# Linear attention and two MLPs: the inverse root by one table function, and a Newton step with one pass less behind it

## The chip, the cores and the metric

The kernel runs on one core of one Trainium2 chip. The metric is the device time of one execution in microseconds (us). The core has five engines that work side by side, each through its own list of instructions in a fixed order: PE (TensorE, matrix products), ACT (ScalarE, table functions and copies), DVE (VectorE, elementwise passes), POOL (GpSimd) and SP (SyncE, which here issues most transfers). An instruction that has to wait for another engine holds up all that stands behind it on its own.

## The reference, cut to what matters

```python
q, k, v: (8, 8, 576, 64)                      # batch, heads, tokens, head size
kv  = einsum('bhsd,bhse->bhde', k, v)
out = einsum('bhsd,bhde->bhse', q, kv)
rms = sqrt(mean(out * out, axis=-1) + 1e-06)
x   = out / rms * g_norm                      # as 4608 x 512
h   = x @ w_in                                # 512 -> 2048
g   = h where h >= 1, 0 where h <= -1, else (h + 1)**2 / 4
x   = g @ w_out                               # 2048 -> 512
return relu(x @ w_in2)**2 @ w_out2            # second MLP
```

The change is in `out / rms`: how 1/rms is made and multiplied in.

## The kernel before, in words

The work goes by batch (8 blocks of 512 tokens; the 64 tokens left of each batch are kept in `xrem` for the end) and by pair of heads (`hp` 0 to 3, 128 rows for two heads). Three stretches follow each other. In the **opening** the attention of batch 0 is made alone (`kv_stage`, `t_first`, `o_first`, `r_first`), pair by pair; while that goes on, the first weight pieces are converted, and PE is given filler products (`pwarm`, L1157). In **layer 1** a loop over blocks and 16 slices of the hidden width runs `h_stage` (12 products into `ph`, then `u`), `g_stage` (split of `u` into a high and a low part, `gs`) and `out_stage` (products into `acc`); the attention of the next batch (`t_stage`, `o_stage`, `r_stage`) is woven in as hooks. The **second stretch** (lines from L794 on) has the last block and the second MLP, and no inverse root.

A float32 operand of a product is split into a high part (a cast, on ACT) and a low part (a subtraction, on DVE). A weight piece goes through four steps first: `raw` (ACT, L268), `d` in two passes (DVE, L270 and L271), then cast (ACT, L217) and subtraction (DVE, L185). The engines of each step are set in the tables ENGINES and ENGINES2 at the head of the file. The order of instructions on each engine is set by a scheduler from the order of the calls and their dependences; `tc.high_priority()` around `o_first` and `r_first` pulls those forward.

The inverse root, for one pair of heads: PE multiplies the squares with `ones` (two halves of 288 columns, `pr`); ACT takes Ln of each half (L535; L602 later), then Exp of -0.5 times that over 576 columns (L537; L604); ACT squares the result into `t` (`square`, L224). DVE then makes one Newton step on it: `newton` twice (L519, one for each half, reading `pr` again), `norm` in two passes over 576 columns (L522 and L523: first with the root `y`, then with `o`, which is the product `out` times -g/2). ACT and DVE split the result into `x`. `r_first` runs four times, `r_stage` 28 times. The table of Ln and Exp is loaded once, at the start (L1146).

PSUM, where products land, has 8 banks. In the opening `ph` of slices 2 to 5 lies in the four banks that `acc` takes over later: the first `acc` product can start only after DVE's pass `u` of slice 2 (L707) has read `ph` out of its bank.

Of the kernel before, what the change touches and what calls it, by code (L numbers as in the profile page):

```python
# [16 lines left out]

LN_SCALE = 2.0**-44  # L20
LN2 = 0.6931471805599453


# [54 lines left out]
def linear_attention_rms_two_mlps(  # L78
# [12 lines left out]
    nc = tc.nc  # L91
# [98 lines left out]
    lnb = const.tile([P, 1], F32, name="lnb")  # L190
    expb = const.tile([P, 1], F32, name="expb")
# [329 lines left out]
    def norm(t, y, o):  # L521
        nc.vector.scalar_tensor_tensor(t, t, -3.0, y, op0=ALU.add, op1=ALU.mult)  # L522
        nc.vector.tensor_tensor(t, o, t, ALU.mult)  # L523
# [3 lines left out]
    def r_first(hp):  # L527
        y, o = og.pop((0, hp))
        t = scratch(hp, "t")
        ms = []  # L530
        for half in range(2):
            ps = bank(0, f"pr_0_{hp}_{half}")
            m = ps[:, :U]
            nc.tensor.matmul(m, ones.bitcast(F32), y[:, half], start=True, stop=True)  # L534
            nc.scalar.activation(y[:, half], m, AF.Ln, bias=lnb, scale=LN_SCALE)  # L535
            ms.append(m)
        nc.scalar.activation(y, y, AF.Exp, bias=expb, scale=-0.5)  # L537
        square(engine("y", 0), t, y)
        for half in range(2):
            newton(t[:, half], ms[half])  # L540
        norm(t, y, o)
        n = TB // 2
        rem = xrem[0][:, hp, :].rearrange("p (h r) -> p h r", h=2)
        nc.gpsimd.tensor_copy(rem, t[:, :, n:])
        x = xs[1, 0][hp].rearrange("p a (h n) -> p a h n", h=2)
        marks.append(split(x, t[:, :, :n], "x", 0))
# [42 lines left out]
    def r_stage(b, hp):  # L589
# [6 lines left out]
        for half in range(2):  # L596
# [5 lines left out]
            nc.scalar.activation(y[:, c], m, AF.Ln, bias=lnb, scale=LN_SCALE)  # L602
            ms.append((c, m))
        nc.scalar.activation(y, y, AF.Exp, bias=expb, scale=-0.5)  # L604
        t = ap1.tile([P, S], F32, tag="wk2", name=f"t_{b}_{hp}")
        square(engine("y", b), t, y)
        for c, m in ms:
            newton(t[:, c], m)
        if b < LAST_B:
            norm(t, y, o)  # L610
# [4 lines left out]
        nc.vector.scalar_tensor_tensor(t, t, -3.0, y, op0=ALU.add, op1=ALU.mult)  # L615
        nc.vector.tensor_tensor(xt, o[:, :TB], t[:, :TB], ALU.mult)
        nc.vector.tensor_tensor(xrem[b][:, hp, :], o[:, TB:], t[:, TB:], ALU.mult)
# [528 lines left out]
    nc.scalar.preload_act_table_set("natural_log_exp_and_others")  # L1146
# [24 lines left out]
    nc.vector.memset(lnb, LN_SCALE * 1e-6)  # L1171
    nc.vector.memset(expb, -22.0 * LN2)
# [122 lines left out]
```

## Time and profile before

| | |
|---|---|
| median of 3 runs | 1556.57 us (1556.27 to 1558.22) |
| the profiled execution's own time | 1556.74 us |
| its span, first to last instruction | 1554.7 us |
| PE busy | 1545.8 us, 99% of the span |
| DVE busy | 1131.3 us, 73% |
| ACT busy | 909.6 us, 59% |

The span is 2.0 us shorter than the time of the same execution; the rest lies around it. The profiled execution stands 0.17 us over the median.

How to read it: busy shares are means over the whole span, and the three stretches are limited by different engines. A busy PE includes the time in which a product that has been issued passes through the array, so short waits can hide in it.

### The profile page before, as it was taken

The numbers are of one execution on the slowest core, as the hardware profiler recorded it, in microseconds if no ns is written. First come the engines' busy times: TensorE is split into PE (matmuls) and PEld (weight loads), VectorE is DVE, ScalarE is ACT, GpSimd is POOL, SyncE is SP. The second block draws the span as 40 slices with busy tenths as digits, with TensorE's granted clock in tenths as the row PEclk, the third lists the DMA queues.
The fourth block names the chain that finished last, engine by engine and source line by source line (L and its number), as shares of the span: only waits on it lengthen the run. The fifth ranks groups of instructions, "written<-read, shape, count | busy, mean of one in ns | idle before, by whom it ended". The sixth has DMA issues, their size and how long they took to land.

```text
span 1554.7 us, 22267 instructions
## 1 busy us (share of the span) xinstructions
PE 1545.8 (99%) x7727; PEld 1283.3 (83%) x7729; DVE 1131.3 (73%) x2000; ACT 909.6 (59%) x1713; POOL 20.5 (1%) x38
## 2 busy tenths in 40 slices
PE   9999999999999999999999999999999999999999
PEld 5787888888888888888888888888888888888898
DVE  6986886877877776754587559778965596558666
ACT  5977766767666676664355346456644463446354
POOL 0000000000000000000000000000000000000000
PEclk9999999999999999999999999999999999999999
DMA  9666899996877967935676867696876676877796
GB/s 288 197 216 187 278 319 279 304 313 197 274 250 238 284 208 227 293 98 172 193 245 194 227 213 246 197 238 200 259 227 204 205 238 197 241 248 224 212 392 249
DMA packets 327519, 368.22 MB, mean 237 GB/s; under 512 B 196976, under 2 KB 222576, under 8 KB 327408
## 3 DMA queue, kind: packets, MB, share of 16 engines
q1 hardware_dynamic: 295360, 308.60, 66.4%
q10 hardware_dynamic: 32048, 58.20, 9.9%
q8 instruction: 61, 1.00, 0.3%
q14 instruction: 50, 0.41, 0.1%
HBM read 282.59 MB, written 84.15 MB: 236 GB/s over the span
## 4 chain that ended last, share of the span: by engine, by line
PE 97%; ACT 1%; DVE 1%; issue 0%; DVEq 0%; ACTq 0%
PE po L878 27%; PE ph L878 27%; PE acc L238 20%; PE ph L238 19%; PE pkv L479 1%; PE po L238 1%; PE pr L601 1%; PE pwarm L1157 1%; ACT raw L268 0%; ACT w L217 0%; PE pr L534 0%; DVE t L519 0%; DVE w L185 0%; PE po L511 0%; DVE t L522 0%; PE po L569 0%
## 5 line engine op out<-in xcount | busy, mean ns | idle before, releaser
L878 PE MATMUL ph<-x,ws 128*128 128x512 f32 (+1 forms) x2016 | 422.4, 371 | 0.0
L878 PEld LDWEIGHTS ph<-x,ws 128*128 128x128 f32 x2016 | 355.8, 188 | 65.6
L878 PE MATMUL po<-t,ws 128*128 128x512 f32 x1680 | 381.6, 389 | 0.0
L878 PEld LDWEIGHTS po<-t,ws 128*128 128x128 f32 x1680 | 315.3, 188 | 65.5
L238 PE MATMUL ph<-x,w 128*128 128x512 f32 x1344 | 329.4, 392 | 1.3 <-ACT w L217 0.6
L238 PEld LDWEIGHTS ph<-x,w 128*128 128x128 f32 x1344 | 248.7, 188 | 54.3 <-ACT w L217 1.5
L807 DVE TENSOR_TENSOR t<-g,t 128x512 fp32r<-128x512 f32 (+1 forms) x288 | 183.3, 641 | 92.2 <-ACT t L217 84.6
L217 ACT CAST t<-g 128x512 fp32r<-128x512 f32 (+1 forms) x288 | 166.5, 585 | 101.8 <-PE po L878 50.2
L238 PE MATMUL acc<-gs,w 128*128 128x512 f32 x696 | 173.0, 392 | 1.5 <-DVE u L707 1.5
L238 PE MATMUL acc<-gs,wt 128*128 128x512 f32 x648 | 157.9, 391 | 0.0
L238 PEld LDWEIGHTS acc<-gs,w 128*128 128x128 f32 x696 | 128.6, 188 | 27.8 <-DVE u L707 1.9
L949 ACT ACTIVATE g<-h 128x512 f32<-128x512 f32 (+1 forms) x120 | 70.7, 589 | 119.8 <-DVE h L938 119.8
L238 PEld LDWEIGHTS acc<-gs,wt 128*128 128x128 f32 x648 | 120.1, 188 | 24.3
L705 ACT ACTIVATE u<-ph,halfb 128x512 f32<-128x512 f32 x112 | 77.2, 690 | 91.5 <-PE ph L238 89.1
L938 DVE CUSTOM_DVE_ANT_0 h<-ph,e 128x512 f32<-128x512 f32 (+1 forms) x120 | 76.4, 638 | 64.8 <-PE ph L878 57.3
L707 DVE SCALAR_TENSOR_TENSOR u<-u,ph 128x512 f32<-128x512 f32 x112 | 76.3, 681 | 54.2 <-ACT u L224 53.8
L928 DVE TENSOR_TENSOR e<-ph,e 128x512 f32<-128x512 f32 (+1 forms) x96 | 61.1, 643 | 50.2 <-PE ph L878 49.6
L230 DVE TENSOR_TENSOR gs<-u,gs 128x512 fp32r<-128x512 f32 x112 | 76.8, 686 | 22.2 <-ACT gs L217 21.8
L217 ACT CAST gs<-u 128x512 fp32r<-128x512 f32 x112 | 69.7, 622 | 37.5 <-DVE u L707 34.7
L224 ACT ACTIVATE u<-u 128x512 f32<-128x512 f32 x112 | 70.8, 632 | 1.4 <-ACT u L705 0.5
L217 ACT CAST x<-xr 128x512 fp32r<-128x512 f32 (+1 forms) x84 | 49.0, 586 | 36.0 <-DVE xr L858 17.5
L807 DVE TENSOR_TENSOR x<-xr,x 128x512 fp32r<-128x512 f32 (+1 forms) x84 | 53.1, 637 | 7.3 <-ACT x L217 7.3
(134 smaller groups left out, 1494.5 us busy)
## 6 DMA issues: line engine op xcount, KB each, us to landing
ws<-wsd SPq DMA_DIRECT2D x336, 512.0 KB, 4.2
wsd<-s ACTq DMA_DIRECT2D x96, 512.0 KB, 4.7
wt<-wsd SPq DMA_DIRECT2D x54, 512.0 KB, 5.4
raw<-in_moe_w_in_dram SPq DMA_DIRECT2D x32, 512.0 KB, 5.8
raw<-in_moe_w_out_dram SPq DMA_DIRECT2D x32, 512.0 KB, 6.2
xr<-x1d SPq DMA_DIRECT2D x36, 256.0 KB, 4.9
out_dram<-ov SPq DMA_DIRECT2D x142, 64.0 KB, 3.5
wsd<-w SPq DMA_DIRECT2D x17, 512.0 KB, 5.0
```

Source lines behind the costliest of these rows:

```text
L217: return e.copy(dst, src)
L224: e.activation(dst, src, AF.Square)
L230: lo = engine(op + "_lo", phase).tensor_tensor(t[:, 1, :], src, t[:, 0, :].bitcast(F32), ALU.subtract)
L238: nc.tensor.matmul(dst, wt(a), xt(c), start=first and n == 0, stop=last and n == 2)
L479: nc.tensor.matmul(ps[s, d], lhs, rhs, start=c == 0, stop=c == MR)
L705: nc.scalar.activation(u, ps, AF.Relu, bias=halfb, scale=0.5)
L707: nc.vector.scalar_tensor_tensor(u, u, 1.0, ps, op0=ALU.min, op1=ALU.max)
L807: engine2(op + "_lo").tensor_tensor(t[:, 1, :], src, t[:, 0, :].bitcast(F32), ALU.subtract)
L878: nc.tensor.matmul(ps, wt(a), xt(c), start=first and n == 0 and i == 0, stop=last and n == len(lhs) - 1 and i == 2, skip_group_check=True,)
L928: nc.vector.tensor_tensor(e[i, p], bank, e[i, 1], ALU.add)
L938: nc.vector._custom_dve(TENSOR_ADD_SAT, out=h, in0=bank, in1=add, s0=float("inf"), s1=0.0)
L949: nc.scalar.activation(g, h, AF.Square)
```

## The change

One function, `Abs_reciprocal_sqrt` of (mean + 1e-6), takes the place of Ln and Exp, and the table loaded at the start is the one that holds it. A new pass on DVE, `o = o * y`, comes ahead of `newton`; `norm` then has one pass, (t - 3) * o, in place of two. For the last batch that one pass writes its two destinations directly.

```diff
-            nc.scalar.activation(y[:, half], m, AF.Ln, bias=lnb, scale=LN_SCALE)
+            nc.scalar.activation(y[:, half], m, AF.Abs_reciprocal_sqrt, bias=epsb)
             ms.append(m)
-        nc.scalar.activation(y, y, AF.Exp, bias=expb, scale=-0.5)
         square(engine("y", 0), t, y)
+        nc.vector.tensor_tensor(o, o, y, ALU.mult)
         for half in range(2):
             newton(t[:, half], ms[half])
-        norm(t, y, o)
+        norm(t, t, o)
...
-    def norm(t, y, o):
-        nc.vector.scalar_tensor_tensor(t, t, -3.0, y, op0=ALU.add, op1=ALU.mult)
-        nc.vector.tensor_tensor(t, o, t, ALU.mult)
+    def norm(dst, t, o):
+        nc.vector.scalar_tensor_tensor(dst, t, -3.0, o, op0=ALU.add, op1=ALU.mult)
...
-        nc.vector.scalar_tensor_tensor(t, t, -3.0, y, op0=ALU.add, op1=ALU.mult)
-        nc.vector.tensor_tensor(xt, o[:, :TB], t[:, :TB], ALU.mult)
-        nc.vector.tensor_tensor(xrem[b][:, hp, :], o[:, TB:], t[:, TB:], ALU.mult)
+        norm(xt, t[:, :TB], o[:, :TB])
+        norm(xrem[b][:, hp, :], t[:, TB:], o[:, TB:])
...
-    nc.scalar.preload_act_table_set("natural_log_exp_and_others")
+    nc.scalar.preload_act_table_set("abs_reciprocal_sqrt_and_small")
```

`r_stage` is changed as `r_first` is. The scheduler lays the instructions out anew. Three places follow. In names such as `t_0_332` and `x_0_1_218` the last number is the buffer's; what stands ahead of it is the pair of heads, or batch (or matrix) and slice. The line numbers of the change are 8 to 11 lower.

First, DVE in the opening, from the pass `o` of pair 1 to the low part of `x` of pair 0. Before:

```order
L211 TENSOR_SCALAR o_1_349<-po_1_1_354,gvec 128x288
L519 SCALAR_TENSOR_TENSOR t_0_332<-pr_0_0_333,t_0_332 128x288
L519 SCALAR_TENSOR_TENSOR t_0_332<-pr_0_1_336,t_0_332 128x288
L185 TENSOR_TENSOR w_0_0_300<-d_0_0_297,w_0_0_300 128x2x256
L522 SCALAR_TENSOR_TENSOR t_0_332<-t_0_332,y_0_282 128x576
L271 SCALAR_TENSOR_TENSOR d_0_1_363<-raw_0_1_153,d_0_1_363 128x512
L523 TENSOR_TENSOR t_0_332<-o_0_283,t_0_332 128x576
```

The same engine and place in the change:

```order
L529 TENSOR_TENSOR o_0_281<-o_0_281,y_0_280 128x576
L511 SCALAR_TENSOR_TENSOR t_0_330<-pr_0_0_331,t_0_330 128x288
L511 SCALAR_TENSOR_TENSOR t_0_330<-pr_0_1_334,t_0_330 128x288
L263 SCALAR_TENSOR_TENSOR d_0_0_295<-raw_0_0_150,d_0_0_295 128x512
L203 TENSOR_SCALAR o_1_346<-po_1_1_351,gvec 128x288
L514 SCALAR_TENSOR_TENSOR t_0_330<-t_0_330,o_0_281 128x576
L178 TENSOR_TENSOR w_0_0_298<-d_0_0_295,w_0_0_298 128x2x256
L529 TENSOR_TENSOR o_1_346<-o_1_346,y_1_345 128x576
L222 TENSOR_TENSOR x_0_0_215<-t_0_330,x_0_0_215 128x512
```

The new product and the Newton passes of pair 0 have moved ahead of `o` of pair 1; the low part of the first weight, `w_0_0`, has moved behind the last pass of pair 0.

Second, ACT around the cast of `x` for pair 1. Before:

```order
L217 CAST x_0_0_217<-t_0_332 128x512
L512 ACTIVATE y_2_409<-po_2_0_411 128x288
L209 ACTIVATE o_2_410<-po_2_0_411,gvec 128x288
L535 ACTIVATE y_2_409<-pr_2_0_431,lnb 128x288
L217 CAST x_0_1_218<-t_1_393 128x512
L512 ACTIVATE y_2_409<-po_2_1_415 128x288
```

In the change:

```order
L209 CAST x_0_0_215<-t_0_330 128x512
L216 ACTIVATE t_1_390<-y_1_345 128x576
L209 CAST x_0_1_216<-t_1_390 128x512
L504 ACTIVATE y_2_405<-po_2_0_407 128x288
L201 ACTIVATE o_2_406<-po_2_0_407,gvec 128x288
```

The cast of `x_0_1` has moved ahead of the squares of pair 2 and of the first table function of pair 2.

Third, DVE where the first `acc` bank is freed (the pass `u` of slice 2). Before:

```order
L707 SCALAR_TENSOR_TENSOR u_0_1_612<-u_0_1_612,ph_0_1_599 128x512
L270 TENSOR_SCALAR d_1_4_635<-raw_1_4_518 128x512
L185 TENSOR_TENSOR w_1_3_596<-d_1_3_593,w_1_3_596 128x2x256
L230 TENSOR_TENSOR gs_0_1_625<-u_0_1_612,gs_0_1_625 128x512
L271 SCALAR_TENSOR_TENSOR d_1_4_635<-raw_1_4_518,d_1_4_635 128x512
L707 SCALAR_TENSOR_TENSOR u_0_2_654<-u_0_2_654,ph_0_2_641 128x512
```

In the change:

```order
L222 TENSOR_TENSOR gs_0_1_619<-u_0_1_606,gs_0_1_619 128x512
L178 TENSOR_TENSOR w_1_3_590<-d_1_3_587,w_1_3_590 128x2x256
L262 TENSOR_SCALAR d_1_4_629<-raw_1_4_512 128x512
L697 SCALAR_TENSOR_TENSOR u_0_2_648<-u_0_2_648,ph_0_2_635 128x512
L263 SCALAR_TENSOR_TENSOR d_1_4_629<-raw_1_4_512,d_1_4_629 128x512
```

The second pass of `d_1_4` has moved from ahead of `u_0_2` to behind it.

## Rows read from the trace of the kernel before

**Rows 1.** the page's head: span, busy us of each engine (share, instructions)

```profile
span 1554.7 us, 22267 instructions
PE 1545.8 (99%) x7727; PEld 1283.3 (83%) x7729; DVE 1131.3 (73%) x2000; ACT 909.6 (59%) x1713; POOL 20.5 (1%) x38
```

**Rows 2.** windows of all engines: stretch, us, busy us (instructions) of each, granted clock, DMA

```profile
27.00:38.00 11.00, 10.25 (x42) 7.34 (x42) 10.20 (x22) 7.51 (x16) 0.64 (x1) 1.00 0.95 330
38.00:57.30 19.30, 17.35 (x88) 12.65 (x87) 18.82 (x35) 18.99 (x37) 0.24 (x1) 1.00 0.91 273
57.30:100.00 42.70, 42.70 (x223) 34.60 (x222) 36.86 (x67) 36.73 (x74) 1.41 (x2) 1.00 0.56 162
100.00:700.00 600.00, 599.82 (x3150) 497.12 (x3148) 451.95 (x832) 411.86 (x817) 15.42 (x22) 1.00 0.80 250
700.00:1550.00 850.00, 850.00 (x4064) 717.55 (x4063) 597.57 (x1004) 421.11 (x747) 0.00 (x0) 1.00 0.74 229
```

**Rows 3.** PE's waits from 80 to 1550 us: waiter, releaser, us, times, longest

```profile
PE ph L238 <- ACT w L217: 0.2, 1, 0.2
```

**Rows 4.** timeline of PE: start, us, what [idle before, releaser]

```profile
1.19 4.73 PE L1157 MATMUL pwarm<-warm 128*128 128x512 bf16 x11 [1.19 <-DVE warm L1152]
...
6.46 1.47 PE L1157 MATMUL pwarm<-warm 128*128 128x512 bf16 x6
...
17.82 1.24 PE L534 MATMUL pr<-y,ones 128*128 128x288 f32 x4 [0.91 <-DVE t L519]
...
53.84 0.97 PE L238 MATMUL acc<-gs,w 128*128 128x512 f32 x3 [1.51 <-DVE u L707]
...
61.53 0.69 PE L479 MATMUL pkv<-v,k 128*64 128x64 f32 x16
```

**Rows 5.** windows of DVE alone: stretch, us, busy us (instructions)

```profile
12.83:53.71 40.88, 37.53 (x75) 1.00 0.95 294
```

**Rows 6.** timeline of DVE, opening: the gaps before u of slice 2

```profile
16.74 0.52 DVE L211 TENSOR_SCALAR o<-po,gvec 128x288 f32<-128x288 f32 x1 [0.98 <-ACT y L512]
...
26.13 0.69 DVE L230 TENSOR_TENSOR x<-t,x 128x512 fp32r<-128x512 f32 x1 [0.75 <-ACT x L217]
...
31.22 0.52 DVE L211 TENSOR_SCALAR o<-po,gvec 128x288 f32<-128x288 f32 x1 [0.67 <-ACT y L512]
...
48.98 0.69 DVE L185 TENSOR_TENSOR w<-d,w 128x512 fp32r<-128x512 f32 x1 [0.32 <-ACT w L217]
...
53.11 0.68 DVE L707 SCALAR_TENSOR_TENSOR u<-u,ph 128x512 f32<-128x512 f32 x1
```

**Rows 7.** timeline of ACT, opening: Ln and what it waits for

```profile
18.61 0.99 ACT L535 ACTIVATE y<-pr,lnb 128x288 f32<-128x288 f32 x2 [0.26 <-PE pr L534]
...
25.09 0.50 ACT L535 ACTIVATE y<-pr,lnb 128x288 f32<-128x288 f32 x1 [1.92 <-PE pr L534]
...
28.89 0.50 ACT L535 ACTIVATE y<-pr,lnb 128x288 f32<-128x288 f32 x1 [1.37 <-PE pr L534]
```

**Rows 8.** ACT's groups by shape: busy us, mean ns, idle before

```profile
L512 ACT ACTIVATE y<-po 128x288 f32<-128x288 f32 x8 | 3.3, 408 | 10.4 <-PE po L511 10.4
...
L535 ACT ACTIVATE y<-pr,lnb 128x288 f32<-128x288 f32 x8 | 3.9, 501 | 3.7 <-PE pr L534 3.7
...
L537 ACT ACTIVATE y<-y,expb 128x576 f32<-128x576 f32 x4 | 3.1, 776 | 0.1
...
L224 ACT ACTIVATE t<-y 128x576 f32<-128x576 f32 x4 | 2.7, 686 | 0.0
```

**Rows 9.** DVE's groups by shape, last passes of the opening

```profile
L522 DVE SCALAR_TENSOR_TENSOR t<-t,y 128x576 f32<-128x576 f32 x4 | 3.0, 753 | 0.0
...
L523 DVE TENSOR_TENSOR t<-o,t 128x576 f32<-128x576 f32 x4 | 3.0, 750 | 0.0
```

**Rows 10.** the raw weights to 75 us: transfers, issue to landing

```profile
DMA to landing us min/median/max: 4.4/8.1/11.2
```

**Rows 11.** the table load: count, ns, first and last start

```profile
L1146 ACT ACT_TABLE_LOAD  x1: 1283/1283/1283, 0.7 to 0.7; - x1
```

More of the change, by code (lines that the diff above doesn't have):

```diff
@@ L16 @@
 BF16 = mybir.dt.bfloat16
-LN_SCALE = 2.0**-44
-LN2 = 0.6931471805599453
 REBIAS = 2.0**-112
@@ L189, in linear_attention_rms_two_mlps @@
     gvec = const.tile([P, 1], F32, name="gvec")
-    lnb = const.tile([P, 1], F32, name="lnb")
-    expb = const.tile([P, 1], F32, name="expb")
+    epsb = const.tile([P, 1], F32, name="epsb")
     halfb = const.tile([P, 1], F32, name="halfb")
@@ L601, in r_stage @@
                 nc.tensor.matmul(m, one, s2[:, c], start=n == 0, stop=n == len(products) - 1)
-            nc.scalar.activation(y[:, c], m, AF.Ln, bias=lnb, scale=LN_SCALE)
+            nc.scalar.activation(y[:, c], m, AF.Abs_reciprocal_sqrt, bias=epsb)
             ms.append((c, m))
-        nc.scalar.activation(y, y, AF.Exp, bias=expb, scale=-0.5)
         t = ap1.tile([P, S], F32, tag="wk2", name=f"t_{b}_{hp}")
         square(engine("y", b), t, y)
+        nc.vector.tensor_tensor(o, o, y, ALU.mult)
         for c, m in ms:
@@ L609, in r_stage @@
         if b < LAST_B:
-            norm(t, y, o)
+            norm(t, t, o)
             nc.gpsimd.tensor_copy(xrem[b][:, hp, :], t[:, TB:])
@@ L1170, in linear_attention_rms_two_mlps @@
     nc.vector.tensor_scalar_mul(gvec, gvec, -0.5)
-    nc.vector.memset(lnb, LN_SCALE * 1e-6)
-    nc.vector.memset(expb, -22.0 * LN2)
+    nc.vector.memset(epsb, 1e-6)
     nc.vector.memset(halfb, 0.5)
```

## The prediction

> **What bounds the kernel now.** I read the head of the page first: PE is busy for 1545.8 of 1554.7 us, so what the change does to ACT and DVE counts only where PE waits for them [rows 1]. The windows say where that is. From 57.3 us on PE is busy without a break: 42.70 of 42.70, 599.82 of 600 and 850 of 850 us, at a granted clock of 1.00, which is the 2.4 GHz level [rows 2]. The waits of PE from 80 to 1550 us are a single one of 0.2 us [rows 3]. Twenty-eight of the 32 inverse roots are made there, on engines that have slack: ACT is busy for 411.86 and DVE for 451.95 of the 600 us from 100 to 700 [rows 2]. Taking 28 Exp away there is worth nothing, since PE's own list of products covers it. If that cover went, 28 Exp at 0.78 us, the opening's price [rows 8], would be 22 us.
>
> That leaves the opening, up to the first `acc` product. Between 38 and 57.3 us ACT is busy for 18.99 and DVE for 18.82 of 19.30 us, PE for 17.35 [rows 2]: here the two elementwise engines set the pace. The last long wait of PE ends it: the `acc` product starts at 53.84 us after 1.51 us of idleness, released by DVE's pass `u` [rows 4], which begins at 53.11 and takes 0.68 us [rows 6]. Whatever makes that pass earlier makes the end earlier by as much, as long as PE, which has no gap behind it, stays fed.
>
> So the question is what holds DVE up before that pass. From 12.83 us (the pass `o` of pair 0, whose inputs the change does not touch) to 53.71, where the engine passes on from `u` of slice 2, DVE is busy for 37.53 of 40.88 us: 3.35 us of gaps [rows 5]. Four of them make 2.72 us: 0.98, 0.75, 0.67 and 0.32, each a wait for ACT [rows 6]. The other 0.63 us is in gaps too short to be listed there.
>
> **The change part by part.** *The root.* No row shows it. Ln, with the same operands (a half of 288 columns out of PSUM, a bias from a column), takes 0.50 us; the square of the same half, without that column, 0.41 [rows 8]. I take 0.50; the bounds are 0.41 and, as if it were an Exp over twice the columns, 0.78. At 0.78 the 8 roots of the opening would cost ACT 8 x 0.28 = 2.2 us more, at 0.41 0.7 us less. The Trainium skill (ScalarE activation tables: per-element evaluation and per-set limits, "What a function is on this engine") says that with the same operands an activation costs the same whichever table is read; by it the 0.50 stands.
>
> *Exp goes.* Four in the opening at 0.78 us: ACT sheds 3.1 us [rows 8]. That is no gain by itself, because DVE does not shed anything.
>
> *DVE.* One pass over 576 columns (L523, 0.75 us) is replaced by the product `o*y` of the same shape and type; the other (L522, 0.75 us) stays with another operand [rows 9]. I take the difference as 0; being four passes of each, a tenth more on one of them would be 4 x 0.075 = 0.3 us. The last batch has the split pass in the other place, with as many columns. What is queued behind the new product on DVE are the two `newton` passes; they need ACT's square of the root, 0.69 us [rows 8], which runs while the product does. So the product delays them by under 0.1 us.
>
> *The gaps, from the order shown.* First gap (0.98, `o` of pair 1 waits for ACT's square of that pair): in the change the product of pair 0 and its `newton` passes stand ahead of it. Exp's place on ACT is taken by the square of the root, so they are ready about 0.7 us after the last root and bring some 0.75 + 0.75 us of work (two halves are one pass of 576 columns). The gap is filled: +0.98. Price: the low part of `w_0_0` now stands behind the last pass of pair 0 on DVE and needs a cast that stands on ACT behind the first root of pair 1. That root's product waited 0.91 us on PE for `newton` [rows 4], which the change lifts, so it starts at 16.9 instead of 17.82; ACT reads it 0.79 us later (18.61 less 17.82 [rows 4, 7]), at 17.7. Root and cast, about 0.9 us, bring the low part to 18.6. DVE gets there at 16.74 + 0.52 + 0.75, about 17.9. A new gap of 0.7.
>
> Second gap (0.75, low part of `x_0_1` waits for its cast): on ACT that cast stood behind a Ln that waited 1.92 us for PE [rows 7]; now it stands ahead of pair 2. +0.75. Third gap (0.67, `o` of pair 3): ACT's square stood behind a Ln that waited 1.37 us for PE [rows 7], and an Exp. The Exp goes, the wait for PE does not, and two new products now wait for roots nearby: I call it unchanged. Fourth gap (0.32): unchanged.
>
> *The pass that moved.* DVE's second pass of `d_1_4` now stands behind `u` of slice 2, and is worth 0.60 us, the time from one 512-column pass to the next (53.71 less 53.11 [rows 5, 6]). It is wanted only for slice 4 of the second matrix, several groups of products later.
>
> *The sum.* 0.98 - 0.70 + 0.75 + 0.60 = 1.63 us if the short gaps all stay; 2.26 us if they go as well. They are hand-overs from ACT, and ACT sheds 3.1 us, so I take 2.2 us. The ends are 0 and 3.35 + 0.60 = 3.95 us, more than which DVE, with its work unchanged, cannot give. Against the profiled execution: 1556.74 - 2.2 = **1554.5 us**, 0.13% under the median of the runs, 1556.57.
>
> *The table.* Square, Relu, Prelu and copies stand between the roots. Before, the trace has one table load, 1.28 us at the start [rows 11]; the order of the change has one too. The Trainium skill (ScalarE: Activation LUTs, "Table sets: the hidden batching unit") says that a switch to a function of another set costs a load, which would speak against a root that shares no set with its neighbours; it also says that cheap functions are in every set, and by that nothing is paid. By the first sentence alone, two loads for each of the opening's four roots would be 8 x 1.28 = 10.3 us, and the time 1564.8; the order shows no such load, and I give it no chance of its own.
>
> **The rivals.**
>
> *More than that (chance 0.22).* All gaps close, because ACT, 3.1 us lighter, is nowhere late: 3.95 us, 1552.8. For it: every listed gap is a wait for ACT [rows 6]. Against it: two of the four go back to ACT's own waits for PE (1.92 and 1.37 us [rows 7]), which stay or only move. It counts as faster by 0.2% (some 3.1 us, about what a measurement of this kernel can tell from no change) from a gain of 3.3 us on the profiled time.
>
> *Hidden anyway (0.08).* `u` comes earlier but PE is then held by something the change does not move: the first product of the woven-in attention, whose keys and values come through SP's queue, or a raw weight. The weights take 4.4 to 11.2 us to land [rows 10]; a transfer issued in its old place that lands at its old time gives all 2.2 us back: 1556.7.
>
> *Slower (0.08): PE's clock.* In the opening PE lives on filler products and short groups. The first 11 fillers take 4.73 us, 0.43 each, the next six 1.47, 0.24 each [rows 4]: half the pace after idleness, that of the 1.2 GHz level. The change moves `qT` of pair 2 behind the Newton step of pair 1 on DVE, and PE's fillers stand ahead of the products that need it, so PE may idle longer there than the 0.91 us now. If the clock fell, each product would take 0.19 us more. By then DVE sets the pace, so the first dozen cost nothing; from about 28 products at half pace (28 x 0.19 = 5.3 us, which is 2.2 + 3.1) the kernel is slower by 0.2%. A plain case is four slices of 12 `ph` products at half pace, 48 x 0.19 = 9.1 us, less PE's 1.95 us of slack from 38 to 57.3 [rows 2] and the 2.2: 5.0 us, 1561.7. Against it: the 0.91 us wait was followed by products at full pace. The Trainium skill (TensorE: Matmul & The Clock Gate, "Part 1: The HAM clock gate") has the half-rate state as the one that idleness leads back to, which is this rival's mechanism.
>
> **How the numbers follow.** The forecast, a gain from 1 to 3.2 us, has 0.62 and its own range of 1553.5 to 1555.7. With the rivals at 0.22, 0.08 and 0.08: faster by over 0.2% is 0.22, slower 0.08, and the rest, 0.70, is within 0.2%. The range of 8 in 10 goes from the bound of the gaps, 1552.8, to no gain at all, 1556.8; it leaves out the slower case and a little on the other side.
>
> **What would show it.** Right: one table load; roots of 0.50 us; no gap of 0.98 before `o` of pair 1 and none of 0.75 before `x_0_1`; a new wait for the cast of `w_0_0` of some 0.7 us; DVE's gaps from its first `o` to `u` of slice 2 down from 3.35 us to between 1.7 and 2.3; the first `acc` product near 51.6 us; PE without a break behind it; the first `pkv` of the second pair, now at 61.53 us [rows 4], earlier by as much. Wrong: gaps of PE after 60 us, roots longer than 0.5 us, products in the opening at 0.43 us, or an `acc` start that moves by 2 us while the end does not.

## The result, and the profile after

The changed kernel takes 1566.09 us (median of 6 runs, 1564.52 to 1571.46) against 1556.79 for the kernel before (6 runs, 1556.27 to 1558.81): a ratio of 1.0064, 95% interval 1.0047 to 1.0082. It is slower by 9.3 us, where 2.2 us of gain were forecast and the range ended at 1556.8. The profiled execution took 1566.26 us, with a span of 1564.4, 9.7 us more than before.

The head of the page after (busy us, share, instructions) answers to [rows 1]:

```profile
span 1564.4 us, 22252 instructions
PE 1549.5 (99%) x7729; PEld 1283.8 (82%) x7729; DVE 1130.4 (72%) x1999; ACT 887.0 (57%) x1681; POOL 16.9 (1%) x38
```

ACT is 22.6 us lighter and has 32 instructions fewer, the 32 Exp; PE has the same 7729 weight loads. The windows of all engines after (stretch, its length, busy us and instructions of PE, PEld, DVE, ACT and POOL, granted clock, DMA share, GB/s) answer to [rows 2]:

```profile
23.00:25.00 2.00, 1.90 (x5) 1.20 (x5) 1.94 (x6) 0.43 (x1) 0.08 (x1) 0.53 1.06 370
25.00:27.00 2.00, 2.00 (x20) 0.95 (x18) 1.05 (x2) 1.74 (x5) 0.00 (x0) 0.62 1.08 385
57.30:100.00 42.70, 42.23 (x218) 33.43 (x217) 35.86 (x65) 33.47 (x70) 0.47 (x2) 1.00 0.60 168
100.00:700.00 600.00, 593.38 (x3115) 490.63 (x3114) 448.17 (x827) 392.96 (x788) 13.18 (x22) 1.00 0.81 249
700.00:1550.00 850.00, 850.00 (x4026) 715.35 (x4025) 597.80 (x1003) 420.24 (x747) 0.00 (x0) 1.00 0.75 230
```

The stretch that had no break now has them: PE is busy for 593.38 of 600 us from 100 to 700, and does 3115 products there where it did 3150 [rows 2]. At 2.72 us for 12 products (below, 545.30 to 548.02) 35 products are 7.9 us; five more are missing from 57.3 to 100 us, 1.1 us. With 0.5 us by which `acc` starts later this estimate makes 9.5 of the 9.7 us. The rest of the kernel, from 700 us, is as full as before. PE's waits from 80 to 1550 us (what waits, what it waits for: us in total, times, longest), of which there was one of 0.2 us [rows 3]:

```profile
PE po L230 <- ACT qT L209: 4.0, 2, 2.4
PE ph L230 <- DVE u L697: 1.0, 1, 1.0
PE ph L230 <- ACT w L209: 0.8, 1, 0.8
PE po L230 <- DVE qT L551: 0.6, 2, 0.4
PE acc L230 <- DVE gs L222: 0.3, 1, 0.3
```

So the loss sits in layer 1, mostly where the attention's products `po` need `qT`. What stands ahead of `qT` is the work on the second MLP's and the last block's weights, which runs beside layer 1: quarters of weights are added (`prep_join`, `prep_sums`) and split into tiles `s` (cast on ACT, L209; subtraction on DVE, L178), which are stored to DRAM (`wsd<-s`); some parts are first loaded back (`wf<-wsd`). The tiles `s` and `wf` share four buffers, so a cast into `s` waits until an earlier store has landed, and a load of `wf` too.

The first of the long stops, in the timeline of ACT after (start us, us, instruction, idle before it and what ended it):

```profile
282.13 0.62 ACT L209 CAST s<-s 128x512 fp32r<-128x512 f32 x1 [4.02 <-DMA wsd<-s]
282.77 0.20 ACT L209 CAST kvbd<-pkv 64x64 fp32r<-64x64 f32 x1
282.88 0.67 ACT L209 CAST qT<-qf 128x576 fp32r<-128x576 f32 x1
```

and in that of PE:

```profile
279.15 2.88 PE L230 MATMUL acc<-gs,w 128*128 128x512 f32 x12
283.61 0.40 PE L230 MATMUL po<-qT,kvbd 128*128 128x288 f32 x1 [1.57 <-ACT qT L209]
...
545.30 2.88 PE L230 MATMUL acc<-gs,w 128*128 128x512 f32 x12
548.02 2.88 PE L230 MATMUL ph<-x,w 128*128 128x512 f32 x12
553.29 0.40 PE L230 MATMUL po<-qT,kvbd 128*128 128x288 f32 x1 [2.39 <-ACT qT L209]
```

ACT stood for 4.02 us at a store that still held the buffer of `s`, with the cast of `qT` two places behind, and PE ran dry for 1.57 us. The longest stop, which ends at 553 us, begins on DVE; its timeline after:

```profile
544.32 0.69 DVE L333 TENSOR_TENSOR wf<-wf 128x512 f32<-128x512 f32 x1 [3.46 <-DMA wf<-wsd]
...
551.76 0.77 DVE L549 STREAM_TRANSPOSE qf<-q 128x576 f32<-128x576 f32 x1
```

DVE stood for 3.46 us at a load, then worked off what had piled up, and came to the transposition of q 7.4 us later; ACT's cast of it ended at 553.2, when PE had been idle for 2.39 us.

The kernel before has these waits too. DVE's and ACT's waits for the two transfers from 57 to 710 us, before:

```profile
DVE wf L341 <- DMA wf<-wsd: 16.8, 7, 3.5
...
ACT s L217 <- DMA wsd<-s: 0.4, 1, 0.4
```

and after:

```profile
DVE wf L333 <- DMA wf<-wsd: 18.7, 7, 7.8
ACT s L209 <- DMA wsd<-s: 6.8, 3, 4.0
```

Seven waits for `wf` cost nothing before. Those of ACT for a store are new, but for 0.4 us. And the cover that PE's list gave before was thin in places. One pair of heads of the kernel before, in the timelines of ACT and of PE:

```profile
565.62 0.67 ACT L217 CAST qT<-qf 128x576 fp32r<-128x576 f32 x1
```

```profile
566.41 0.33 PE L238 MATMUL po<-qT,kvbd 128*128 128x288 f32 x1
```

The cast ends at 566.29 and the product that needs it starts at 566.41, 0.12 us later, without a break on PE. Worked out in the same way for all 26 pairs that have such a cast, eight had less than 0.95 us between the two.

The opening, in PE's timeline after, answers to [rows 4]:

```profile
22.04 0.81 PE L1147 MATMUL pwarm<-warm 128*128 128x512 bf16 x3 [1.16 <-DVE t L511]
...
23.90 2.13 PE L503 MATMUL po<-qT,kv 128*128 128x288 f32 x4
...
54.37 2.35 PE L230 MATMUL acc<-gs,w 128*128 128x512 f32 x9
```

After 1.16 us of idleness four `po` take 2.13 us; other groups of four in this trace take 1.13. The windows above give a clock of 0.53 for that stretch, close to the lower level, 1.2 GHz. DVE's timeline there answers to [rows 6]:

```profile
17.77 0.52 DVE L203 TENSOR_SCALAR o<-po,gvec 128x288 f32<-128x288 f32 x1
...
19.29 0.69 DVE L178 TENSOR_TENSOR w<-d,w 128x512 fp32r<-128x512 f32 x1 [0.34 <-ACT w L209]
...
26.51 0.52 DVE L203 TENSOR_SCALAR o<-po,gvec 128x288 f32<-128x288 f32 x1 [0.95 <-ACT y L504]
...
31.33 0.76 DVE L529 TENSOR_TENSOR o<-o,y 128x576 f32<-128x576 f32 x1 [0.59 <-ACT y L526]
```

And DVE's windows from its first `o` to the pass `u` of slice 2 (us, busy us), as [rows 5]:

```profile
13.86:54.23 40.37, 36.96 (x73) 0.96 1.02 289
```

The root itself is as forecast: 503 ns in the group of the eight roots of the opening (Ln: 501 [rows 8]), and one table load.

```profile
L526 ACT ACTIVATE y<-pr,epsb 128x288 f32<-128x288 f32 x8 | 4.0, 503 | 2.8 <-PE pr L525 2.8
```

### The profile page after: what moved, and what is told of

Same layout as the page of the kernel before. It is cut to its first block, busy times and chain, and to the rows that moved or that the text cites. A ratio compares the mean times of both kernels' runs of the same rounds, so it can differ in the third digit from the quotient of the medians.

```text
span 1564.4 us, 22252 instructions
## 1 busy us (share of the span) xinstructions
PE 1549.5 (99%) x7729; PEld 1283.8 (82%) x7729; DVE 1130.4 (72%) x1999; ACT 887.0 (57%) x1681; POOL 16.9 (1%) x38
## 4 chain that ended last, share of the span: by engine, by line
PE 78%; DMA 2%; DVE 1%; ACT 0%; issue 0%; SPq 0%; DVEq 0%; ACTq 0%
PE po L868 27%; PE ph L868 27%; PE acc L230 11%; PE ph L230 11%; DMA wf<-wsd 1%; PE po L230 1%; PE pkv L471 1%; PE pr L592 1%; DMA wsd<-s 0%; DMA x1d<-ev 0%; DVE u L697 0%; DVE qf L549 0%; DVE s L178 0%; ACT qT L209 0%; ACT s L209 0%
## 5 line engine op out<-in xcount | busy, mean ns | idle before, releaser
L209 ACT CAST t<-g 128x512 fp32r<-128x512 f32 (+1 forms) x288 | 165.5, 585 | 94.4 <-DVE t L797 48.2
L209 ACT CAST gs<-u 128x512 fp32r<-128x512 f32 x112 | 69.8, 623 | 46.6 <-DVE u L697 40.9
L209 ACT CAST x<-xr 128x512 fp32r<-128x512 f32 (+1 forms) x84 | 49.0, 586 | 47.2 <-DVE xr L848 22.1
```

What stands on the lines that cost most here:

```text
L209: return e.copy(dst, src)
```

## The experiments

Theory A: the loss comes from layer 1. With Exp gone there the scheduler lays ACT's and DVE's lists out anew, so that casts and joins of the weight preparation come at a transfer that has not landed, and `qT` or `u` stands behind them. Rival B at first: the opening (clock, table) or the extra product makes the loss. Later, when single mends did not help, B became: any list laid anew has such stops, whichever wait is mended; and a theory C was set beside A: what counts is the place of `qT` and the root in the lists, not the transfer. Each expectation says which is meant. All results in one table; "before" is the kernel before on the same chip, "stops" the sum of PE's waits from 60 us to the end and "store" ACT's waits, with a cast of `s`, for `wsd<-s` from 57 to 710 us; both are of the one profiled execution, which in e9, e11 and e19 took 5.3, 4.6 and 2.8 us more than the median beside it.

| run | us | ratio, 95% interval | stops, us | store, us |
|---|---|---|---|---|
| before | 1556.79 | 1 | 0.2 | 0.4 |
| after | 1566.09 | 1.0064 (1.0047 to 1.0082) | 6.7 | 6.8 |
| e1_opening_only | 1559.43 | 1.0013 (1.0003 to 1.0022) | 2.1 | none |
| e2_layer1_only | 1566.12 | 1.0059 (1.0044 to 1.0074) | 4.9 | 5.0 |
| e3_product_only | 1559.45 | 1.0012 (1.0003 to 1.0022) | 0.8 | none |
| e4_root_only | 1566.98 | 1.0063 (1.0048 to 1.0078) | 6.6 | 8.6 |
| e5_reversed_halves | 1556.82 | 0.9998 (0.9989 to 1.0007) | none | none |
| e7_store_earlier | 1567.43 | 1.0061 (1.0046 to 1.0077) | 5.9 | 4.7 |
| e8_copy_for_exp | 1560.94 | 1.0024 (1.0015 to 1.0034) | 3.3 | 1.4 |
| e9_join_later | 1567.32 | 1.0070 (1.0051 to 1.0088) | 10.9 | 7.0 |
| e10_split_on_gpsimd | 1598.25 | 1.0265 (1.0250 to 1.0281) | 25.1 | none |
| e11_o_one_step_later | 1572.69 | 1.0105 (1.0089 to 1.0121) | 12.2 | 8.1 |
| e12_o_later_store_earlier | 1573.82 | 1.0110 (1.0095 to 1.0125) | 12.6 | 5.3 |
| e13_opening_product_behind | 1566.20 | 1.0062 (1.0045 to 1.0079) | 6.5 | 5.9 |
| e14_fifth_buffer | 1561.04 | 1.0024 (1.0014 to 1.0034) | 3.8 | 1.7 |
| e15_qT_first | 1568.50 | 1.0068 (1.0051 to 1.0084) | 7.0 | 4.7 |
| e16_attention_first | 1581.89 | 1.0158 (1.0143 to 1.0173) | 11.9 | 1.8 |
| e17_qT_and_root_first | 1563.59 | 1.0042 (1.0026 to 1.0057) | 2.7 | none |
| e18_root_first_from_2 | 1563.01 | 1.0035 (1.0021 to 1.0048) | 2.9 | 3.7 |
| e19_before_root_first | 1562.39 | 1.0032 (1.0019 to 1.0045) | 5.1 | 1.4 |

### Which part of the change

**The opening alone** (`r_first` as changed, `r_stage` as before; since layer 1 keeps Ln and Exp, their table is loaded again behind the opening).

```diff
 # r_first only
-            nc.scalar.activation(y[:, half], m, AF.Ln, bias=lnb, scale=LN_SCALE)
+            nc.scalar.activation(y[:, half], m, AF.Abs_reciprocal_sqrt, bias=epsb)
...
-        nc.scalar.activation(y, y, AF.Exp, bias=expb, scale=-0.5)
```

> The change in the opening alone (four roots); layer 1 keeps Ln and Exp and both passes, with one more table load in between. Theory A (the loss lies in layer 1, where ACT and DVE stand at a transfer of the weight preparation with attention work queued behind it; the opening gives at most 2 us of it): 1556 to 1559 us, no wait of ACT for the store of s over 1 us. Rival B (the opening's late po of pair 2 and the half-rate clock behind it cost the bulk): 1563 to 1567 us. Both expect the stretch of granted clock near 0.5 around 23 to 27 us again, if it comes from the order.

**Layer 1 alone** (`r_stage` as changed, `r_first` as before).

```diff
 # r_stage only
-            nc.scalar.activation(y[:, c], m, AF.Ln, bias=lnb, scale=LN_SCALE)
+            nc.scalar.activation(y[:, c], m, AF.Abs_reciprocal_sqrt, bias=epsb)
...
-        nc.scalar.activation(y, y, AF.Exp, bias=expb, scale=-0.5)
```

> The change in layer 1 alone (28 roots), the opening as before, one table load more. Theory A: 1561 to 1566 us, with waits of PE for qT or u between 100 and 600 us that sum to 4 us or more, behind waits for transfers of s or wf. Rival B: 1556 to 1558 us, PE without waits behind 60 us.

**The product and the one pass alone** (Ln and Exp kept everywhere).

```diff
+        nc.vector.tensor_tensor(o, o, y, ALU.mult)
...
-        nc.vector.scalar_tensor_tensor(t, t, -3.0, y, op0=ALU.add, op1=ALU.mult)
-        nc.vector.tensor_tensor(t, o, t, ALU.mult)
+        nc.vector.scalar_tensor_tensor(t, t, -3.0, o, op0=ALU.add, op1=ALU.mult)
```

> The product of o and the root ahead of the Newton step and the one pass behind it, with Ln and Exp kept. If the lighter ACT (28 Exp fewer) is what re-lays the preparation against the attention, this is 1556 to 1559 us; if DVE's new pass ahead of newton does it, 1562 to 1567 us.

**The root alone** (one table function everywhere, DVE's passes as before).

```diff
-            nc.scalar.activation(y[:, c], m, AF.Ln, bias=lnb, scale=LN_SCALE)
+            nc.scalar.activation(y[:, c], m, AF.Abs_reciprocal_sqrt, bias=epsb)
...
-        nc.scalar.activation(y, y, AF.Exp, bias=expb, scale=-0.5)
 # norm() keeps its two passes
```

> The one table function in place of Ln and Exp, with the passes on DVE as before. If the lighter ACT re-lays the preparation against the attention: 1562 to 1567 us with waits for stores of s or loads of wf ahead of waits of PE; if it is DVE's new pass: 1554 to 1558 us.

Measured: 1559.43, 1566.12, 1559.45 and 1566.98 us. The two runs that take Exp out of layer 1 have the whole loss, whether DVE's passes are changed or not; the two that leave it there lose 0.12 to 0.13%. Each is within 0.5 us of A's range. So A's place holds: the opening with its table, and the extra product, make 0.13% and 0.12% (at most 0.22% by their intervals). The waits of PE in the run with layer 1 alone:

```profile
PE po L239 <- ACT qT L218: 3.1, 1, 3.1
PE ph L239 <- DVE u L709: 1.4, 1, 1.4
```

are again at `qT` and `u`. In both runs ACT waits for stores (5.0 and 8.6 us); in the other two it does not.

**A control: the same work, the two Newton halves in reverse order.**

```diff
-        for c, m in ms:
+        for c, m in ms[::-1]:
             newton(t[:, c], m)
```

> The kernel before, with the two Newton halves of each head pair issued in reverse order in both the opening and layer 1: the same work, and an order of instructions that differs from that of before only around those halves. A control for the two runs near 1559.4 us (the opening alone and the product alone). Theory A (the loss comes from where ScalarE and VectorE stand at a transfer while TensorE runs dry, so a re-laid order costs only where it makes such a stop): 1556.5 to 1557.5 us and no stop of TensorE over 0.5 us behind 60 us. Rival B (any departure from the old order costs about 2 us): 1558.5 to 1560 us.

1556.82 us, no stop at all: a change of order alone costs nothing when it moves little. Here nothing but the two halves changed places, so the run does not try a list laid anew; the last of the priority runs below does.

### Is it ScalarE's lighter load?

**A copy of the root onto itself in Exp's place, in layer 1.**

```diff
             ms.append((c, m))
+        nc.scalar.copy(y, y)
```

> The changed kernel, with a copy of the root's 576 columns onto itself on ScalarE in layer 1, where the Exp stood (the opening stays without it): ScalarE is as busy in layer 1 as before, with the new table function. Theory A (the loss comes from the lighter ScalarE, which lays the weight preparation's casts in other places): 1557 to 1561 us, as the run that kept Ln and Exp with the new product, and no stop over 1 us behind 200 us. Rival B (the new function or its way of waiting makes the stops): 1564 to 1567 us. Between these, 1561 to 1564 us, the order of this kernel has stops of its own.

1560.94 us, at the upper edge of A's range and outside B's: 5.2 us come back from an instruction that does nothing. ACT's wait for stores falls from 6.8 to 1.4 us and the stops at `qT` go. The "no stop over 1 us" was too much: one at `kvbd` of 1.4 us is left, and two of about 1 us at 121 and 132 us. So the new function is not to blame for that part. But the copy also gave a new list: DVE has 1427 of its 1999 passes in the order of the changed kernel, ACT 1321 of 1681. The run does not tell ACT's load from the place that each instruction got.

### Mending the wait

**Stores one step earlier.**

```diff
-            owe(2, dst, t[:, hs])
+            owe(1, dst, t[:, hs])
```

> The changed kernel, with one edit: the transfers that store the prepared weight halves (tile s) are issued one step earlier, so that their buffers come free sooner and the loads of wf behind them start sooner. Theory A (the stops of TensorE at 283, 321 and 553 us are ScalarE and VectorE standing at those stores and loads, with qT and u queued behind): at least two of the three stops go, ScalarE's wait for wsd<-s falls from 6.8 to under 3 us, and the time falls to 1558 to 1562 us. Rival B (the stops come with the new order whatever the transfers do): 1564 to 1567 us, with the same three stops. Rival C (an earlier issue stands on ScalarE's queue before the cast that it stores is made, so it moves the wait to ScalarE): above 1567 us.

1567.43 us. Of the three stops only that at `u` went. At 280 us the cast of `s` still stood for 3.41 us with `qT` behind it. The time lies 0.4 us above B's range, without the longer wait of ACT that C named (4.7 us, 6.8 after). A's numbers failed: a store that is due a step earlier did not land early enough for the cast behind it.

**The join and what hangs on it one step later.**

```diff
-            (9, 1, prep_join, ()),
-            (10, 1, prep_sums, ()),
-            (10, 1, prep_split, (2,)),
-            (11, 1, prep_split, (3,)),
+            (10, 1, prep_join, ()),
+            (11, 1, prep_sums, ()),
+            (11, 1, prep_split, (2,)),
+            (12, 1, prep_split, (3,)),
```

> The changed kernel, with the join of the stored halves (wf), its sums and its two splits one step later in the list of preparation work, and the load of wf where it was: VectorE comes to wf some 3 to 5 us later. Theory A: VectorE's waits for wf fall from 18.7 to under 8 us, the stop at 321 us goes, the one at 553 us shrinks, the one at 283 us (a store, not a load) may stay; 1560 to 1563.5 us. Rival B (the stops come with the new order whatever the transfers do): 1564 to 1567 us with stops of the same sum, about 6 us.

1567.32 us; DVE's waits for `wf` rose to 20.7 us in place of falling. The load is issued when a buffer comes free, and what frees it (splits and their stores) was put later too; that this is why is argued, not shown. A's sum failed again. The time is 0.3 us above B's range, with more stops than B named (10.9 us).

**The casts of `s` on GpSimd.**

```diff
-    "s_hi": "A",
+    "s_hi": "P",
```

> The changed kernel with the upper half of each prepared weight split (tile s, some 80 casts of 128x512) made on GpSimd in place of ScalarE, so that no cast which waits for a store stands ahead of qT on ScalarE. Theory A (TensorE stops at 283 and 553 us because qT is queued in order behind such a cast): the two stops at qT go; if GpSimd does not hold VectorE up, 1557 to 1562 us. Rival B (qT is late for another reason, such as wf on VectorE ahead of qf): the stop at 553 us stays, over 2 us, and the time stays over 1563 us. Rival C (GpSimd's casts are so slow that the stores and so the loads of wf come later): VectorE's waits for wf rise over 25 us and the time over 1567 us.

1598.25 us. The wait for a cast of `s` did not go, it changed engines. DVE's wait for these casts from 57 to 710 us, and PE's largest waits:

```profile
DVE s L178 <- POOL s L205: 17.5, 18, 5.0
```

```profile
PE po L230 <- ACT qT L209: 13.8, 5, 5.5
PE po L230 <- DVE qT L551: 4.1, 6, 1.1
```

The subtraction that follows a cast is on DVE; ahead of one of the five stops at `qT` on ACT it stood for 5.0 us with `qf` behind it. Ahead of the other four, the longest (5.54 us, to 478.16) among them, DVE stood at a load of `wf` instead, which is the reason that B named:

```profile
474.22 0.69 DVE L333 TENSOR_TENSOR wf<-wf 128x512 f32<-128x512 f32 x1 [3.52 <-DMA wf<-wsd]
```

C's price held, its mark (longer waits for `wf`) did not: they fell to 15.4 us.

**`po` one step later**, and the same **with the earlier stores.**

```diff
-                (s + 3, o_stage, b, hp, 0),
-                (s + 4, o_stage, b, hp, 1),
+                (s + 4, o_stage, b, hp, 0),
+                (s + 5, o_stage, b, hp, 1),
```

> The changed kernel with the products po of layer 1's attention one step (some 2.7 us of TensorE's work) later in the program, and everything else where it was: qT may come 2.7 us later without a stop. Theory A: the stops at qT (4.0 us together, and the lower clock behind them) go or fall under 1 us, the one at u at 321 us may stay; 1559 to 1562.5 us. Rival B (a stop that is taken away at qT comes back at pr, which now has one step less behind po): stops of over 3 us in sum at pr or at another place, 1564 to 1567 us.

> Both the run with po one step later and the run with the stores one step earlier in one kernel; the earlier store alone took away the stop at u (321 us), and left those at qT. Theory A: no stop over 1 us behind 200 us; 1557.5 to 1561 us. Rival B (the stops only move): as the run with po later alone, or above it, 1563 us and over.

1572.69 and 1573.82 us, the first above the ranges of both. With `po` later alone the stops at `qT` on ACT shrink from 4.0 to 0.3 us, as A said, and come back larger at the next link, as B said; with the earlier stores as well, one of 3.5 us stands at `qT` again. PE's waits of the first of the two:

```profile
PE pr L592 <- DVE s2lo L578: 6.1, 4, 2.6
PE pr L592 <- ACT wk L201: 2.0, 3, 0.8
```

**A fifth buffer for `s` and `wf`** (its room is taken from the pool `st`, 5 tiles in place of 7).

```diff
-    prep_tags = itertools.cycle(range(NF - TAIL + RING + 2, NF))
+    prep_tags = itertools.cycle([*(f"w1_{i}" for i in range(NF - TAIL + RING + 2, NF)), "more"])
...
-    st = ctx.enter_context(tc.tile_pool(name="st", bufs=7))
+    st = ctx.enter_context(tc.tile_pool(name="st", bufs=5))
```

> The changed kernel with a fifth buffer of 4 KB a partition for the prepared halves s and the loaded wf; its room is taken from the pool of k, v and the evicted tiles (5 buffers in place of 7). Theory A (the casts of s stand at the store that still holds their buffer, and wf's load starts when such a store has landed): ScalarE's wait for wsd<-s falls from 6.8 to under 2 us, VectorE's wait for wf from 18.7 to under 10 us, and the stops of TensorE behind 200 us from 5.9 to under 2.5 us in sum; 1558 to 1562.5 us. Rival B (the stops come with any list laid anew): stops of 4 us or more in sum, 1563.5 us or more. The smaller pool may make k and v late, which would show as stops at pkv.

1561.04 us, in A's range: 5.1 us come back. This list is nearly that of the changed kernel (DVE has 1912 of 1999 passes in the same order, ACT 1636 of 1681), so it is the room for transfers, and hardly the list, that gives them back. ACT's wait for the store, in the list of its waits from 57 to 710 us:

```profile
ACT s L209 <- DMA wsd<-s: 1.7, 1, 1.7
```

and PE's:

```profile
PE ph L230 <- DVE u L697: 1.4, 1, 1.4
PE po L230 <- ACT qT L209: 0.8, 1, 0.8
```

The stops at `qT` on ACT fell from 4.0 to 0.8 us. DVE's waits for `wf` did not fall as expected (15.5 us, one of 8.2): that part of A was wrong, and the stop at `u` stays. The stops behind 200 us sum to 2.6 us, just over A's 2.5.

### Mending the place in the list

**Priority** for `t_stage`; for all of layer 1's attention; for `t_stage` and `r_stage`; for these two from batch 2 on; and the last of these in the kernel before. The second to fourth have the opening of the run with the product behind, below. The diff is that of the last two.

```diff
         for f, a in hooks.get((t, 0), []):
-            f(*a)
+            if f in (t_stage, r_stage) and a[0] >= 2:
+                with tc.high_priority():
+                    f(*a)
+            else:
+                f(*a)
```

> The changed kernel with the transposition and split of q in layer 1 (t_stage) given priority over the rest, so that qT stands ahead of the casts of s in ScalarE's list where the scheduler can put it there. Theory C (qT's place behind a waiting cast is the cause): the stops at qT go (4.6 us in the changed kernel), the one at u may stay; 1559.5 to 1563 us. Rival B (the list laid anew has other stops): the stops at qT go or not, and the sum behind 200 us stays at 4 us or more; 1563.5 to 1568 us.

> The changed kernel with all four parts of layer 1's attention given priority over the rest, and the product behind the Newton halves in the opening. Theory C: no stop at qT, pr or pkv behind 100 us over 0.5 us; the casts of s and gs come later, which TensorE covers; 1556 to 1560 us. Rival B: what is put behind now makes the stops: gs or u late for acc and the next ph, 4 us or more in sum, above 1562 us.

> As the run before it, but with priority for t_stage and r_stage alone; the products po and pkv and their evictions stay where the list puts them. Theory C: between the run with qT alone and the run with all of the attention, 1557 to 1562 us, without a stop at qT over 0.5 us. Rival B: stops of 4 us or more in sum at po, pr or u, 1563 us or more.

> The changed kernel with the product behind the Newton halves in the opening, and priority for t_stage and r_stage from batch 2 on (batch 1 as in the changed kernel, so that the split of layer 1's weights is not pushed back). Theory C (the loss was qT and the root standing behind waiting casts in the in-order lists): no stop of TensorE over 0.5 us behind 150 us, stops of at most 1.5 us before, no clock under 0.99 in any hundred us; 1557 to 1560 us, level with the kernel before within 0.2%. Rival B (a list laid anew with the lighter ScalarE loses its 4 us or more wherever it is mended): over 1562 us. Faster than 1554 us would need a gain that covered work cannot give, and neither expects it.

> The kernel before with nothing changed but the same priority for t_stage and r_stage from batch 2 on. Theory C: TensorE has no stop to lose there, so the priority gives nothing and the wider slack costs nothing: 1556 to 1558.5 us. Rival B (any new list costs): stops of 1 to 4 us, 1559 to 1563 us.

1568.50, 1581.89, 1563.59, 1563.01 and 1562.39 us. `qT` alone does not mend it (4.2 us of stops at `qT` stay). All of the attention ahead makes `gs` and `v` late, and leaves 3.3 us of stops at `qT`, where C expected none. With `qT` and the root ahead there is no stop at `qT` left; PE's waits of that run, all of them:

```profile
PE ph L230 <- ACT w L209: 1.6, 1, 1.6
PE ph L230 <- DVE u L698: 0.9, 1, 0.9
PE acc L230 <- ACT w L209: 0.2, 1, 0.2
```

They lie between 121 and 133 us, where layer 1's own weights `w` are still being split and now come later. From 200 us on its windows are as full as before (100.00 of 100, 99.92, 100.00, 100.00, 100.00 in the five stretches of 100 us). So with `qT` and the root ahead the stops behind 200 us go, as C says. Whether their place does it is not shown: ACT's waits for a store are gone in this run too, as A would have it. The time, 1563.59, is above C's range (four runs, 1560.92 to 1567.09). Nearly all of the loss is there by 144 us: DVE empties the first bank of `acc` at 144.3 us, before at 139.0. The stops are only part of it, for behind the first of them the clock fell:

```profile
120.00:125.00 5.00, 3.77 (x11) 3.08 (x12) 3.42 (x6) 3.15 (x8) 0.00 (x0) 0.66 0.00 0
```

The kernel before does 24 products in that stretch, at 1.00. Priority from batch 2 on was to spare the weights: the stop at `w` falls to 0.8 us, and two new ones at `pr` (1.7 us, at 210 and 213 us) take its place. C's time failed; B's forecast, over 1562 us, held, with stops of 2.9 us in sum.

The last run decides more than it was meant to. In the kernel before, where nothing was to be mended and ACT has all its Exp, the same priority costs 0.32%, in B's range; DVE has 1581 of 2000 passes in the old order, ACT 1403 of 1713. PE's waits there, but for one of 0.2 us:

```profile
PE pr L601 <- DVE s2lo L587: 2.2, 1, 2.2
PE pr L601 <- ACT wk L209: 2.0, 1, 2.0
PE po L238 <- DVE qT L560: 0.7, 1, 0.7
```

With that priority in both, the changed kernel (1563.01, with the product behind in the opening) and the kernel before (1562.39) are level within their intervals, some 0.13% each.

### The opening

**The product behind the Newton halves, in the opening alone.**

```diff
-        nc.vector.tensor_tensor(o, o, y, ALU.mult)
         for half in range(2):
-            newton(t[:, half], ms[half])
+            last = newton(t[:, half], ms[half])
+        with tc.issue_after(last.ins):
+            nc.vector.tensor_tensor(o, o, y, ALU.mult)
```

> The changed kernel with the product o*y put behind the two Newton halves in the opening alone; layer 1 keeps its order nearly row for row (VectorE 1984 of 1996 rows). The Newton halves are what frees the banks of pr for TensorE's fillers at 22 us. Theory A for the opening (the fillers wait for the bank 1.16 us, TensorE's clock falls and the next po take twice their time): the wait at 22 us falls under 0.6 us, the first acc product starts at 52.3 to 53.8 us in place of 54.37, and the time falls by 0.5 to 2 us, to 1564 to 1565.6 us. Rival B (the opening is set by the chain of k and v and by ScalarE's work, not by that bank): the first acc product starts at 54 us or later, and the time stays at 1566 us. Layer 1 in both: the same stops at about 283, 321 and 553 us, 5 to 7 us together, since it keeps its order.

1566.20 us. `acc` starts at 52.83 us, as A said, and the clock from 21 to 27 us is 1.00. But the wait that was to fall under 0.6 us is one of 1.39, now at `kv`, and the time is B's. The run with earlier stores, whose opening is that of the changed kernel, shows why this says little: there the clock held too. Its windows (of all engines, then of DVE alone from its first `o` to `u` of slice 2):

```profile
23.00:25.00 2.00, 2.00 (x13) 0.99 (x13) 1.97 (x5) 1.06 (x4) 0.00 (x0) 1.00 1.05 378
...
13.72:52.66 38.94, 36.88 (x74) 1.00 1.02 293
```

The same instructions that took 40.37 us in the profiled execution after took 38.94 there.

## Why the prediction was wrong

**The step that failed** is in the second sentence from the end of its first paragraph: "Taking 28 Exp away there is worth nothing, since PE's own list of products covers it." Worth nothing it was not: the runs that take it away carry the whole loss (1.0063 with the root alone, 1.0012 with the product alone), as stops of PE in layer 1. The sentence read "PE never waits" as "there is room". The trace of before had shown both things that were missing: DVE stood at a transfer of `wf` seven times, for 16.8 us, without harm, and in eight of 26 pairs `qT` was ready less than 0.95 us before its product. Such a list fits the transfers by a narrow margin. The prediction looked at what the order did to the opening and not at what it did to layer 1, and priced a lost cover only as Exp's own time (22 us), not as ACT and DVE standing at a transfer with `qT` behind.

**What is shown, and how far.** The loss lies in layer 1 and comes with the lists made without Exp. Half of it goes through the four buffers: a fifth gives back 5.1 us with nearly the same list. A useless copy in Exp's place gives back 5.2 us, but with a new list. So "a lighter ACT costs 9 us" is too strong. The last priority run shows that a list laid anew loses 5 us with the heavier ACT as well, and on such lists the two kernels are level. That is one pair of lists: that Exp by itself is worth nothing, as forecast, fits it and is not shown beyond it. What is shown is that the list which the scheduler makes for the changed kernel is 9 us slower. Mends that moved one link by a step (stores, join, `po`, casts on another engine, `qT`) took away the stops they were aimed at in part or not at all, or found others.

**The opening, term by term.** The root at 0.50 us, the one table load, DVE's difference of 0 (product 754 ns for 750 [rows 9]) and the pass that moved (DVE busy for 36.96 in place of 37.53 us [rows 5]) came as forecast. One load agrees with the sentence of the Trainium skill (ScalarE: Activation LUTs, "Table sets: the hidden batching unit") by which cheap functions cost no switch. The first gap is filled, the new one at `w_0_0` is 0.34 us for 0.7, since the cast was done 0.4 us earlier than forecast (the terms for DVE's arrival add up to 18.0, not 17.9). The second gap is gone. The third did not stay as it was: `o` of pair 3 waits only 0.17 us, but `o` of pair 2, behind the four slow `po`, has a new wait of 0.95, and a product `o*y` waits 0.59 for its root. DVE's gaps came to 3.41 us, against 1.7 to 2.3 in the forecast. Where the clock held (the run with earlier stores) they were 38.94 - 36.88 = 2.06, and the stretch took 38.94 in place of 40.88 us: a gain of 1.94 us, for 2.2 forecast. So the sum was right for an opening at full clock, in part by luck: the short gaps, 0.63 us before, which the step from 1.63 to 2.2 us took to go, stayed (2.06 less the three gaps listed in that run, 0.34, 0.58 and 0.39, is 0.75 us).

**The rival on the clock** named the place (`qT` of pair 2 behind the Newton step of pair 1, PE's fillers ahead of it) and was given 0.08. It came: 1.16 us of idleness, then half pace. Its price was too high, 40.37 - 38.94 = 1.4 us against 5.0, since DVE set the pace soon after. Another 1.03 us comes ahead of all that: DVE's first `o` stands at 13.86 us, not at 12.83 [rows 5]. Most of it is there when the first `pkv` starts, 6.61 us after and 5.84 before; in the four executions with the opening of before that start lies between 5.8 and 7.3 us, so nothing speaks for the change as its cause.

**And the opening's gain is not kept.** The run with the opening alone held its clock, had its `acc` start 39.62 us after the first `o` for 41.01 before [rows 4, 5], and still took 1559.43 us. Its first `o` stood 1.69 us later in the profiled execution, and its later list has stops of 1.8 us at `pr` and `u`, at 120 and 131 us, that before has not.

**Still open:** why the run with priority from batch 2 on stays 5.7 us above before with only 2.9 us of stops and the clock at 1.00 where they stand; what makes the half of the loss that the fifth buffer leaves; and whether there is an order in which the opening's 1.9 us stay. No version that was run beats the kernel before.

## What to carry to other kernels

A bottleneck engine without a break tells that its inputs are in time, not by how much: before calling a saving on another engine covered, read the smallest distances between an input's end and its use, and the waits for transfers that do no harm yet. Where a scheduler orders the instructions, a change of one engine's load can change every list, and here, where inputs came just in time, the new list was the larger term. Run a control that moves the list and not the work, before giving a saving or a loss to the instruction that was edited.

## What the runs showed of the hardware

A short stop can cost more than its idleness. In the run with layer 1 alone PE waited 3.05 us for `qT` at 551.55 us, and the windows (us, busy us of the engines, granted clock in the third column from the end) are:

```profile
547.00:551.00 4.00, 1.50 (x7) 0.92 (x5) 3.65 (x7) 1.94 (x4) 0.31 (x1) 1.00 0.34 135
551.00:555.00 4.00, 3.45 (x9) 2.75 (x10) 3.13 (x5) 3.85 (x9) 0.00 (x0) 0.58 0.46 77
555.00:559.00 4.00, 4.00 (x20) 3.35 (x20) 2.30 (x4) 2.62 (x6) 0.00 (x0) 1.00 0.76 259
```

Nine products in the 4 us from 551 on, at 0.58, then twenty in the next 4. The changed kernel's own stop of 2.39 us at the same place left the clock at 1.00, with 16 products from 553 to 557 us. In the opening, the same list met a lower clock in some executions and not in others: with the product ahead of the Newton halves the clock fell between 21 and 27 us in 8 of 10 profiled executions, with the product behind in none of 4. The counts are small, and no run was made to settle it; nor is the product needed for it, since with the root alone, which has no such product, the clock fell as well (0.63 and 0.52 from 23 to 25 and 25 to 27 us), and with the product alone it held. Whole executions say the same of the price: of the six of the changed kernel the shortest, 1564.52 us, has a mean granted clock of 1.000 and the longest, 1571.46, one of 0.996. The Trainium skill (TensorE: Matmul & The Clock Gate, "Part 1: The HAM clock gate") says that how many products run slowly varies from run to run of one kernel; the two windows of the one opening list that two kernels share, 0.53 and 1.00 from 23 to 25 us, agree.
